# A linear-attention and gated-layer kernel: when the norms of four row tiles are asked for at the end of the second attention layer

## The chip, the cores and the metric

The kernel runs on one core of a Trainium2 chip. A core has five engines that run side by side and wait for each other through semaphores: TensorE (PE) multiplies matrices into the banks of PSUM, VectorE (DVE) and ScalarE (ACT) work on rows in SBUF and PSUM, GpSimd (POOL) works on SBUF, and SyncE (SP) issues most of the transfers (DMAs). The metric is the time of one execution on the device in microseconds (us); lower is better.

## The reference, cut to what matters

Four layers follow each other on x of 2048 rows by 1024 columns. Layers 0 and 2 are linear attention with 32 heads, layers 1 and 3 a gated feed-forward layer of width 3584. Each takes a layer norm of x and adds its result to x.

```
x = x + _A_ref(_layernorm(x), A_wqkv, A_wo)               # layer 0
x = x + _B_ref(_layernorm(x), B_W_gate, B_W_up, B_W_down) # layer 1
x = x + _A_ref(_layernorm(x), A_wqkv, A_wo)               # layer 2
x = x + _B_ref(_layernorm(x), B_W_gate, B_W_up, B_W_down) # layer 3

_layernorm(x) = (x - mean(x)) / sqrt(var(x) + 1e-5)       # per row
_A_ref: pq, pk = phi(q), phi(k);  kv = sum_s pk v;  z = sum_s pk
        o = (pq kv) / (pq z + 1e-6);  returns o @ wo
_B_ref: h = relu(x W_gate) * (x W_up);  returns h @ W_down
```

The place of the change is the end of layer 2 and the start of layer 3: the rows that layer 2 has just completed are normed for layer 3.

## The kernel before

**Tiles.** x lies in SBUF as 16 tiles of 128 rows (tile t), four of which are a quarter. Layer 2 ends with the product of the scaled queries `pqT` and the matrix `T` (the folded output weights). For quarters 0 and 1 `out_unit` (L792) makes one half of a tile at a time: eight matmuls into one PSUM bank, which DVE then adds onto x with `add_up` (L787; its instruction stands under L788), summing the row as it does so. Quarter 0 runs by columns, first the left halves of tiles 0 to 3 and then the right halves, quarter 1 by rows. Quarter 2 is made in pairs of tiles by `products` (L836), a scheme of seven products numbered m = 1, 5, 2, 6, 3, 7, 4, which saves matmuls by adding blocks before and after (`sums_T` and `sums_q` make the blocks, under L553). Quarter 3 waits for layer 3 to run.

**Banks.** The units of quarters 0 and 1 and four banks of `products` share a pool of four PSUM banks, so that a unit can start only when DVE has emptied the bank of the unit four before it. Two more banks, `oy`, take the products m = 6, 7 and 4 in turn.

**The norm of a tile** has four parts. `ln_norm_sums` (L217) lets DVE make the negative mean from the row sums of both halves (L224), and ACT the sum of squares (L227), then Ln and Exp (L228, L229) for `rstd`. Its inner `scale` makes the scaled rows `xnb`: for tiles 1 to 4 of layer 3 on DVE (L233), for the others on ACT (L236, L237). `ln_turn` (L411) has SP issue a DMA that transposes them into `xnT` (L416). With tile j of quarter 0 and tile 4 + j of quarter 1 both transposed, `sums_x` (L1150) adds and subtracts their blocks on DVE (L1160 to L1163). `glu` (L1172) reads `xnT` and these sums.

**What sets the order.** `_Later` (L71) holds tasks by tick; every output unit of L974 and of the loop at L975, and each of the seven products of quarter 2, is followed by one tick, and tasks due at one tick run in the order in which they were registered. `ln_at` (L418) asks for a tile's statistics after `delay` ticks, for its scaling one tick later and for its transpose `lag` ticks after that; `ln_later` (L434) does so for four tiles, `step` ticks apart. On DVE and POOL the order of these requests is the order of the instructions, since `manual_schedule` covers this stretch (L950). On PE, ACT and SP a planner orders the instructions by its own estimate of when each is ready; where two are ready the one asked for first goes first. Every engine runs its list in order.

Between the same ticks SP is given other transfers. `free_slowly` (L967) loads layer 3's first weights at ticks 1, 3 and 5 after L967 (gate weights under L1083, their block sums under L1086). `bring` (L959) fetches tiles of x that had been sent to DRAM, two each at what are ticks 5 and 7 after L973 (L279). The norms of quarter 1 are asked for at L978, at ticks 7, 9, 11 and 14 counted from L973, and `sums_x` at ticks 16, 18, 20 and 21 (L979). The first sums of the left-over blocks stand at ticks 1, 3 and 5 (L971).

Of the kernel before, what the change touches and what calls it, by code (L numbers as in the profile page):

```python
# [92 lines left out]
class _Net:  # L93
# [380 lines left out]
    def layer_A(self, l, last_ln):  # L474
# [253 lines left out]
        def z_mult(sc, j):  # L728
            prod = ksum
            nc.gpsimd.tensor_tensor(out=prod, in0=pq_of[sc, j], in1=zrow, op=ALU.mult)  # L730
            if l and sc == self.NQ - 1:
                later.at(6, lambda: self.behind(self.last_put, lambda _: z_sum(prod, sc, j), (0,)))
            else:
                later.at(2, lambda: z_sum(prod, sc, j))
# [26 lines left out]
        def q_turn(sc, j):  # L761
            if sc not in pqT:
                pqT[sc] = self.slot(f"pqT{l}_{sc}")
            self.last_turn = nc.sync.dma_start_transpose(out=pqT[sc][:, :, j * P:(j + 1) * P],
                                                         in_=pq_of[sc, j])

        def fold_wo(n):

            n2, a = divmod(n, H)
            if n2 == 0:  # L770
                T.append(self.slot(f"T{l}_{a}", [P, 4, D]))
            ps = [pool.tile([P, NW], F32, tag=tag, name=f"fold{l}_{n}_{i}") for i, (pool, tag) in
                  enumerate(((self.kvp, "kv0"), (self.kvp, "kv1"), (self.ps3, "b"), (self.ps3, "b")))]
            wo = ring.get((l, f"o{n2}"))
            for b in range(R):
                g = a * R + b
                for i in range(R):
                    e = slice(i * HD, (i + 1) * HD)
                    nc.tensor.matmul(ps[i][b * HD:(b + 1) * HD, :], lhsT=kvT[e, g, e],
                                     rhs=wo[e, g, :], start=True, stop=True,  # L780
                                     tile_position=(i * HD, b * HD))
            for i in range(R):
                g = a * R + i
                dst = T[g // 4][:, g % 4, n2 * NW:(n2 + 1) * NW]
                nc.scalar.activation(out=dst, in_=ps[i], func=ACT.Copy)
# [90 lines left out]
        def column_major(f, q):  # L876
            return [lambda j=j, c=c: f(q, j, c) for c in range(H) for j in range(QT)]

        def row_major(f, q):
            return [lambda j=j, c=c: f(q, j, c) for j in range(QT) for c in range(H)]  # L880

        def run(*lists):

            n = max(len(u) for u in lists)
            for i in range(n):
                for u in lists:
                    if i < len(u):
                        u[i]()
                        later.tick()
# [60 lines left out]
        with self.tc.manual_schedule(engines={mybir.EngineType.DVE, mybir.EngineType.Pool}):  # L950
            q3 = row_major(q_unit, self.NQ - 1)
            out0 = column_major(out_unit, 0)
            bring = self.bring_back if l else self.load_x
            ring.load_to(ring.index((l, "v1")) + 1)
            m_products(q3.pop(0))
            q3.insert(0, lambda: None)
            later.at(1, lambda: self.behind(ring.last, bring, range(self.NS)))
            for t in range(self.NS, self.ST - QT, 2):
                later.at((8 if l else 10) + t, lambda t=t: self.behind(self.last_turn, bring, (t, t + 1)))  # L959

            def with_fold(u, i):
                return lambda: (u(), fold_wo(i // 2) if i % 2 == 0 else None)

            run(q3[:2])
            run([with_fold(u, i) for i, u in enumerate(q3[2:] + out0[:1])])
            run(out0[1:3])
            ring.free_slowly((l, "o0"), later, 2)  # L967
            sums_T, sums_q, products = out_pairs()
            for i in range(11, 11 if l else self.ST):
                later.at(1 + 3 * (i - 11), lambda i=i: z_mult(*divmod(i, QT)))  # L970
            for n, at in enumerate((1, 3, 5) if l else ()):  # L971
                later.at(at, lambda n=n: self.behind(self.last_x, sums_T, (n,)))
            self.ln_later(last_ln, 0, 2, 2, 2)  # L973
            run(out0[3:])  # L974
            for sc in range(1, self.NQ - 1):  # L975
                if sc == 1:
                    for j in range(QT):
                        self.ln_at((2, 4, 6, 9 if l else 8)[j], last_ln, QT + j, 2, lambda j=j: self.last_seed if l and j == 3 else None)  # L978
                        later.at((11 if l else 12, 13, 15, 16)[j], lambda j=j: self.behind(  # L979
                            self.last_x, lambda j: self.sums_x(last_ln, 0, j), (j,)))  # L980
                if sc == 1 and l == 0:
                    for w, n in (("g", 3), ("u", 11)):
                        later.at(n, lambda w=w: self.behind(
                            self.last_x, lambda w: self.make_gu(ring.get((last_ln, 0, w, 0)), w, 0), (w,)))
                if sc == 1 or l == 0:
                    for n in range(4 if l else 0):
                        later.at(3 + n, lambda n=n: self.behind(self.last_x, lambda n: sums_q(2, (n,)), (n,)))
                    run(row_major(out_unit, sc))
                else:
                    self.behind(self.last_x, sums_T, (3,))  # L990
                    products(sc, 1)
            self.pairs = (lambda ns: [sums_T(n) for n in ns], lambda: sums_q(self.NQ - 1),
                          lambda: products(self.NQ - 1, 2))
            self.late_z = [lambda j=j: z_mult(self.NQ - 1, j) for j in range(QT)] if l else []
            self.turns = [lambda j=j: q_turn(self.NQ - 1, j) for j in range(QT)] + [
                lambda t=t: self.behind(self.last_turn, bring, (t,)) for t in range(self.ST - QT, self.ST)]
# [606 lines left out]
```

## Time and profile before

| What | us |
|---|---|
| median of 3 runs | 1450.57 (1449.26 to 1451.74) |
| the profiled execution | 1449.07 |
| its span, first to last instruction | 1447.3 |
| PE busy | 1437.4 |
| DVE busy | 964.6 |
| ACT busy | 606.7 |
| POOL busy | 312.1 |

The profile is one execution, taken by the hardware's profiler; its span is 1.8 us shorter than its time, because something lies before the first and after the last instruction. Times in the views are counted from the start of the span. A line of the order of time gives the start, the length, the engine, the line of the kernel, the operation and the tiles (out<-in); square brackets give how long the engine had stood idle and what ended it. "SPq" marks SP's queue: its length is the time that the issue held SP, not the transfer's.

### The profile page before, as it was taken

To read this page: it belongs to the slowest core of one execution; us is meant where nothing else is said; L and a number is where in the kernel's file an instruction comes from. 1 tells how busy PE (TensorE), PEld (TensorE's weight loads), DVE (VectorE), ACT (ScalarE), POOL (GpSimd) and SP (SyncE) were. 2 spreads that over 40 slices of the span, in tenths; PEclk is the share of its full clock that TensorE was granted. 3 is DMA by queue.
4 is the path that set the end of the run, shared out by engine and by line. 5 is a ranking of instruction groups with operands and counts; after the bars stand their busy time and mean duration, and the time that the engine had idled before them with its cause. 6 is when DMAs were issued, how large, how long until landed. Compare 5 with 4: busy or idle time off the path is not lost.

```text
span 1447.3 us, 20243 instructions
## 1 busy us (share of the span) xinstructions
PE 1437.4 (99%) x7422; PEld 708.0 (49%) x7422; DVE 964.6 (67%) x1795; ACT 606.7 (42%) x1101; POOL 312.1 (22%) x221
## 2 busy tenths in 40 slices
PE   9999999999999999999999999999999999999998
PEld 4444444444455444445654444444444574444457
DVE  7978698777594456549678876855545864444595
ACT  7872563333333334332068626532333433333300
POOL 1453861011100011110031587040111011111002
PEclk9999999999999999999999999999999999999999
DMA  9950787898469999636973119859843799444465
GB/s 285 238 161 8 175 210 209 278 338 262 157 219 307 352 290 306 201 128 222 295 238 95 59 30 254 241 168 327 254 146 129 218 296 323 146 145 146 153 234 181
DMA packets 328836, 304.90 MB, mean 211 GB/s; under 512 B 107456, under 2 KB 291776, under 8 KB 327712
## 3 DMA queue, kind: packets, MB, share of 16 engines
q1 hardware_dynamic: 320688, 282.30, 65.3%
q10 hardware_dynamic: 6560, 17.24, 3.1%
q0 software_dynamic: 1488, 4.07, 0.8%
q8 instruction: 58, 0.95, 0.3%
q14 instruction: 42, 0.34, 0.1%
HBM read 227.28 MB, written 51.64 MB: 193 GB/s over the span
## 4 chain that ended last, share of the span: by engine, by line
PE 92%; DVE 4%; ACT 2%; issue 1%; DMA 1%; POOL 0%; DVEq 0%; ACTq 0%
PE ps L500 11%; PE yu L1187 10%; PE yg L1187 10%; PE dy L1307 8%; PE xu L1187 7%; PE xg L1187 7%; PE dx L1307 6%; PE vg L1187 3%; PE zu L1187 3%; PE zg L1187 3%; PE vu L1187 3%; PE my L582 3%; PE dyT L1359 2%; PE mx L582 2%; PE mv L582 2%; PE dy L1359 2%
## 5 line engine op out<-in xcount | busy, mean ns | idle before, releaser
L1187 PEld LDWEIGHTS <-w 128*128 128x128 f16 (+1 forms) x3136 | 306.7, 98 | 372.5 <-issue 3.7
L1247 POOL TENSOR_TENSOR h<-m5u,m5g 128x512 f16<-128x512 f32 x56 | 73.0, 1303 | 717.3 <-DVE m5u L1243 615.2
L500 PE MATMUL ps<-w,xnT 128*128 128x512 bf16 x768 | 170.0, 379 | 0.5 <-ACT xnT L354 0.2
L1230 DVE TENSOR_TENSOR zg<-yg,m5g 128x512 f32<-128x512 f32 x56 | 39.1, 699 | 195.3 <-PE yg L1187 191.4
L500 PEld LDWEIGHTS <-xnT 128*128 128x128 bf16 x768 | 74.2, 98 | 90.4 <-issue 1.8
L1187 PE MATMUL xu<-xnT,w 128*128 128x512 f16 x448 | 115.1, 379 | 0.0
L1187 PE MATMUL yu<-s,w 128*128 128x512 f16 x448 | 114.9, 379 | 0.1
L1187 PE MATMUL xg<-xnT,w 128*128 128x512 f16 x448 | 115.0, 379 | 0.0
L1187 PE MATMUL yg<-s,w 128*128 128x512 f16 x448 | 114.9, 379 | 0.0
L1307 PEld LDWEIGHTS <-h 128*128 128x128 f16 x672 | 65.8, 98 | 78.2
L1359 PEld LDWEIGHTS <-h 128*128 128x128 f16 x966 | 94.5, 98 | 12.3
L443 ACT ACTIVATE e<-e,eps 128x512 f32<-128x512 f32 x128 | 91.0, 720 | 3.2
L730 POOL TENSOR_TENSOR kvc<-pq,kvc 128x1024 f32<-128x1024 bf16 x32 | 78.5, 2454 | 58.0 <-DVE den L744 35.1
L1195 ACT ACTIVATE m5g<-m5g 128x512 f32<-128x512 f32 x56 | 35.1, 627 | 124.2 <-DVE m5g L1243 124.2
L1307 PE MATMUL dx<-w,h 128*128 128x512 bf16 x392 | 85.3, 379 | 0.0
L1211 ACT ACTIVATE m5g<-vg 128x512 f32<-128x512 f32 x56 | 33.4, 597 | 100.9 <-PE vg L1187 100.9
L521 POOL TENSOR_TENSOR kvc<-kvc,slab 128x512 f32<-128x512 f32 x46 | 57.2, 1250 | 76.0 <-DVE slab L446 72.7
L1198 DVE TENSOR_TENSOR h<-yu,r 128x512 f16<-128x512 f32 x56 | 38.6, 690 | 50.3 <-PE yu L1187 50.3
L796 PE MATMUL ps<-T,pqT 128*128 128x512 bf16 x320 | 69.7, 379 | 0.0
L1195 ACT ACTIVATE r<-yg 128x512 f32<-128x512 f32 x56 | 33.4, 597 | 84.8 <-PE yg L1187 84.8
L1195 ACT ACTIVATE r<-zg 128x512 f32<-128x512 f32 x56 | 32.8, 586 | 80.9 <-PE zg L1187 73.3
L442 ACT ACTIVATE e<-ps 128x512 f32<-128x512 f32 x92 | 54.3, 590 | 29.2 <-PE ps L500 28.3
(238 smaller groups left out, 2405.6 us busy)
## 6 DMA issues: line engine op xcount, KB each, us to landing
w<-in_B_W_gate_dram SPq DMA_DIRECT2D x56, 512.0 KB, 6.6
w<-in_B_W_up_dram SPq DMA_DIRECT2D x56, 512.0 KB, 5.9
w<-tg SPq DMA_DIRECT2D x42, 512.0 KB, 7.5
w<-tu SPq DMA_DIRECT2D x42, 512.0 KB, 6.6
w<-ddT SPq DMA_DIRECT2D x21, 896.0 KB, 6.5
w<-td SPq DMA_DIRECT2D x18, 896.0 KB, 5.2
w<-dd SPq DMA_DIRECT2D x15, 896.0 KB, 5.4
w<-in_B_W_down_dram SPq DMA_DIRECT2D x14, 896.0 KB, 4.8
```

What stands on the lines that cost most here:

```text
L442: nc.scalar.activation(out=e, in_=ps, func=ACT.Relu, scale=-1.0)
L443: self.last_exp = nc.scalar.activation(out=e, in_=e, func=ACT.Exp, scale=-1.0, bias=self.eps6[:, 0:1])
L500: nc.tensor.matmul(by_row(ps), lhsT=self.xnT[l, l_q][:, kt, j * P:(j + 1) * P], rhs=w[:, kt, :].rearrange("p (b i d) -> p i b d", i=R, d=H ...
L521: nc.gpsimd.tensor_tensor(out=ksum[:, cols], in0=ksum[:, cols], in1=pk, op=ALU.add)
L582: nc.tensor.matmul(banks[j], lhsT=A(i)[:, j * P:(j + 1) * P], rhs=B(i), start=start and i == 0, stop=i == NS - 1, skip_group_check=True)
L730: nc.gpsimd.tensor_tensor(out=prod, in0=pq_of[sc, j], in1=zrow, op=ALU.mult)
L796: nc.tensor.matmul(ps, lhsT=pqT[sc][:, g, j * P:(j + 1) * P], rhs=T[g // 4][:, g % 4, n2 * NW:(n2 + 1) * NW], start=(g == 0), stop=(g == G ...
L1187: nc.tensor.matmul(ps, lhsT=W[w][m][:, k, :], rhs=A[m][:, k, :], start=start and k == 0, stop=k == 3, skip_group_check=True)
L1195: self.last_relu = nc.scalar.activation(out=out, in_=ps, func=ACT.Relu)
L1247: self.last_h = nc.gpsimd.tensor_tensor(out=h[:, 3, :], in0=V["u"], in1=V["g"], op=ALU.mult)
L1307: nc.tensor.matmul(banks[j], lhsT=A(k)[:, j * P:(j + 1) * P], rhs=w[:, i, :], start=start and k == 0, stop=k == self.U - 1, skip_group_che ...
L1359: nc.tensor.matmul(bank[:, j * H:(j + 1) * H], lhsT=A[i // 2][:, i % 2, j * P:(j + 1) * P], rhs=B[m][:, i, :], start=start and i == 0 and ...
```

## The change

One call is changed. In layer 2 alone (`l` is 2; in layer 0 the old values stay) the four tiles of quarter 0 are asked for one tick apart, at ticks 2, 3, 4 and 5 in place of 2, 4, 6 and 8, and each transpose one tick after the scaling in place of two. The scalings so move from ticks 3, 5, 7, 9 to 3, 4, 5, 6 and the transposes from 5, 7, 9, 11 to 4, 5, 6, 7.

```
-            self.ln_later(last_ln, 0, 2, 2, 2)
+            self.ln_later(last_ln, 0, 2, 1 if l else 2, 1 if l else 2)
             run(out0[3:])
```

`run(out0[3:])` holds the last five units of quarter 0, so that ticks 1 to 5 follow these and ticks 6 to 13 the units of quarter 1.

## The prediction

> **What bounds the kernel now.** I read four views in this order: the page's busy line, the waits of TensorE (PE) around the change, VectorE's (DVE's) instructions in order of time there, and SyncE's (SP's) queue. The busy line says how much can be gained at all:
>
> ```profile
> PE 1437.4 (99%) x7422; PEld 708.0 (49%) x7422; DVE 964.6 (67%) x1795; ACT 606.7 (42%) x1101; POOL 312.1 (22%) x221
> ```
>
> PE is busy for 1437.4 of 1447.3 us, so an edit counts only where PE stands still. PE's waits from 890 to 940 us (engine and line <- what it waited for: total, times, longest):
>
> ```profile
> PE oy L864 <- DVE x L852: 1.8, 1, 1.8
> PE oy L864 <- DVE x L788: 0.5, 1, 0.5
> PE ov L864 <- DVE x L788: 0.4, 1, 0.4
> PE ox L864 <- DVE x L788: 0.2, 1, 0.2
> ```
>
> All are waits for DVE to empty a PSUM bank. By the starts of the matmuls, 0.216 us apart when nothing holds them, PE loses 0.19, 0.35 and 0.59 us at 916.7, 917.9 and 919.4, then 1.95 at 928.2 and 0.66 at 932.1: 3.74 us, 0.26% of the span. That is the most a perfect edit of this place can give. DVE's order of time shows what makes it late (start, length, what; in brackets its idle time before):
>
> ```profile
> 906.53 0.81 DVE L233 TENSOR_SCALAR xnb<-x,mv,rstd 128x1024 f16<-128x1024 f32 x1 [0.33 <-ACT rstd L229]
> ...
> 910.98 0.81 DVE L233 TENSOR_SCALAR xnb<-x,mv,rstd 128x1024 f16<-128x1024 f32 x1 [2.05 <-ACT rstd L229]
> ...
> 923.01 0.69 DVE L788 SCALAR_TENSOR_TENSOR x<-ox,x 128x512 f32<-128x512 f32 x1
> ...
> 926.00 0.42 DVE L1160 TENSOR_TENSOR s<-xnT 128x512 f16<-128x512 f16 x1 [2.29 <-DMA xnT<-xnb]
> ```
>
> Twice DVE stands before a scaling (L233) for ScalarE's (ACT's) rstd, 2.38 us together; then, with its adds done at 923.70, 2.29 us for a transpose to land before the first sums of layer 3 (L1160). The adds behind that wait (L852) hold PE at 928.2. SP's queue:
>
> ```profile
> 907.72 0.90 SPq L279 DMA_DIRECT2D x<-away  x2
> 908.72 0.64 SPq L1083 DMA_DIRECT2D w<-in_B_W_gate_dram  x1
> 909.40 1.42 SPq L1086 DMA_DIRECT2D w<-tg  x1
> 910.93 3.85 SPq L416 DMA_TRANSPOSE xnT<-xnb  x1
> 914.82 1.05 SPq L279 DMA_DIRECT2D x<-away  x2
> 915.97 12.38 SPq L416 DMA_TRANSPOSE xnT<-xnb  x7
> ```
>
> The transpose of tile 0, whose scaled rows ACT had finished at 904.79, goes out only at 910.93, behind the loads asked for before it. The eight go in the order of their ticks, 0, 1, 2, 4, 3, 5, 6, 7; the first sums need tiles 0 and 4. By the trace's semaphore updates the fourth, tile 4, was issued at 921.17 and landed at 925.91.
>
> [...] all loads and transposes from 906 to 930 us landed in the order of issue, so a transpose moved ahead pushes what it overtakes back. [...] the squares (L227) took 1148. [...] The trace has such a packet at 923.56 (934 ns), and the transposes' packets nearly stop from 924.1 to 925.3. [...] here it fell on tile 4's transpose.
>
> **The change part by part.** It adds and removes no instruction. Ticks are output units from L973 on. Statistics of tiles 0 to 3 go from ticks 2, 4, 6, 8 to 2, 3, 4, 5, scalings from 3, 5, 7, 9 to 3 to 6, transposes from 5, 7, 9, 11 to 4, 5, 6, 7.
>
> *DVE, whose order is written out.* Before, an add and a 1.59 us sum (L553) stood between mean 1 (L224, 903.88) and scaling 1 (906.53). Now scaling 1 follows an add and mean 2, ready at about 904.3. It needs rstd 1. ACT must still do tile 0's shift and scaling (0.29 + 1.24) and square 1 (1.15 + 0.19), Ln (0.29) and Exp (0.20): from 903.2 that is 906.5, as now. But mean 2 is there by then, and the planner does not put Ln straight behind its square when another square is ready: squares of tiles 2 and 4 at 908.11 and 909.26 both ran before their Ln at 910.39. I take the same here: square 1 at 904.70 plus the 2.87 us from 908.11 to scaling 2 at 910.98 gives scaling 1 at 907.6, idle 3.3 us; bounds 905.3 (square 1 before tile 0's scaling) and 907.8. Then the add and sum run, mean 3 ends at 910.6, and scaling 2 has its rstd: idle 0. Scaling 3 has only scaling 2 (0.73) and an add (0.65) behind mean 3; its chain needs 1.9: idle 0.55. Scaling 4 has an add and a sum (1.3) behind its mean: idle 0.65, where it had none. Sum of DVE idle: 4.5 against 2.38, so DVE is 2.1 us later at the last out_unit add (919.22 becomes 921.3).
>
> *Who waits for that.* Behind each scaling on DVE stand the adds that free PE's four banks. Unit (4,0) is drained at 911.9 instead of 907.95 and unit (6,0) on its bank wanted to start at 909.59: PE loses about 2.2 us there that it does not lose now, and the products (L864) start 2.1 to 2.2 later.
>
> *What it hides behind.* Before, DVE reached the first sums at 923.70 and stood until 926.00. Now it arrives at 923.70 + 2.2 = 925.9. The stall is paid at the scalings instead of at the transpose. If this cover were gone (tile 4 already landed before), the 2.2 us would be a plain loss.
>
> *SP and the DMAs.* All eight transposes still go out; tile 0's passes four transfers (two bring-backs, gate weights and their sums), tiles 1 and 2 pass the second pair of bring-backs, tile 3 passes tile 4. Service times from the packets: transposes 0.92 us, bring-backs 1.3, gate weights 1.75, sums 1.3. From 911.25, when the up weights are through: tile 0 912.2, two bring-backs 914.8, gate and sums 917.9, tiles 1 and 2 919.8, two bring-backs 922.4 (landed 923.2; 921.24 before), tile 3 923.3, tile 4 924.3, landed about 925; with the pause up to 926.3. So tile 4, now fifth in line, is hardly earlier than 925.91. The delayed bring-backs feed L852, which DVE now reaches at about 923.3: hidden, by 0.1 us; without DVE's lag they would hold it. The weights passed are for later units: hidden. POOL's queue is not touched.
>
> *Sum.* First sums at 926.0 (before 926.00); sums 1.47, first L852 0.68: the bank is free at 928.2 (before 928.15), but PE ends the products before it at 919.36 + 2.2 + 4 x 1.73 = 928.5, so m = 7 starts at 928.5 (928.21). The last product waits for the DVE chain from the first sums, 932.1 as before. PE's losses up to m = 7: 0.19 + 0.35 + 0.59 + 1.95 = 3.08 before, 1.13 + 2.2 = 3.3 after, of which the shorter wait of the last product gives most back. Between 0 and +0.3 I take +0.1: span 1447.4, execution 1449.2 against 1449.07; the median shown, 1450.57, is 1.5 above the profiled execution, so 1450.7. Bounds: first sums at 925.0 (rstd 1 early, tile 4 landing without the pause) give -1.0; at 927.0 (DVE's wait longer, or the pause on tile 4) +1.0.
>
> **Rivals.** (a) Faster: the transposes do come early and DVE no longer waits. For: SP sat on tile 0 for 6 us, and the pause may move off tile 4. Against: tile 4 stays behind the same bytes, and the second bring-backs land later. It saves the 1.95 us at 928.2: 1448.6; with the smaller stalls up to all 3.74: 1446.8. (b) Slower, small: ACT puts another square ahead of rstd 3 and rstd 4 too, 3.1 us from mean to scaling as for tile 2, +1.0 each: 1452.6. (c) Slower: SP holds tile 4. A transpose issued behind a full queue took 1.88 to 3.85 us on SP instead of 1.25. With tiles 2 and 3 just ahead, tile 3 may take 3.85 from 919.6 and tile 4 3.12, then 3.5 to land as before: 930.1 instead of 926.0, all paid by PE behind L852: +4.1, 1454.7. It decides from a landing at 928.9 on. Against: the bytes ahead are through by 923. (d) The planner keeps the old order of SP and ACT: 1450.6.
>
> **How the numbers follow.** A measurement of this kernel can tell about 0.2%, 2.9 us, from no change. Likeliest case 0.58, own range 1449.6 to 1451.7; (a) 0.18, of which 0.08 beyond 2.9 us; (b) 0.10; (c) 0.11; (d) 0.03. So faster 0.08, slower 0.11, same 0.81. Cutting off most of (c) and the far part of (a) leaves 1448.0 to 1453.6.
>
> **What would show it.** Right: idle of about 3 us before the first L233 and little before L1160, out units of PE waiting for L788 from about 909.6, no wait for L852 at m = 7. Tile 0's transpose at about 907.7, the second bring-backs after tiles 1 and 2. Wrong: L233 waits under 1 us, or tile 4 landing before 924 or after 928, or another order of PE between products and layer 3's first matmuls, which could fill PE's stall.

## The result and the profile after

The changed kernel takes 1452.51 us (median of 22 runs, 1451.20 to 1453.82) against 1450.38 us before (22 runs, 1448.94 to 1451.74). The ratio is 1.0015 with a 95% interval of 1.0009 to 1.0022: 2.1 us slower. That is clear of the noise, but below the 0.2% that the prediction set as its bound for "no change". The profiled execution took 1452.42 us, with a span of 1450.6 us, against 1449.07 and 1447.3 before. The predicted time was 1450.7 us. One execution of the last kernel below, which took 2166.26 us at a mean clock of 0.654, is left out of all comparisons.

The busy line of the page, after:

```profile
PE 1439.2 (99%) x7422; PEld 708.7 (49%) x7422; DVE 964.5 (66%) x1795; ACT 606.3 (42%) x1101; POOL 312.0 (22%) x221
```

The instruction counts are those of before. TensorE (PE) is 1.8 us busier with the same 7422 matmuls, so some of them took longer. PE's waits from 890 to 940 us, the same stretch as before (engine and line <- what it waited for: total, times, longest):

```profile
PE oy L864 <- DVE x L852: 2.2, 1, 2.2
PE ps L796 <- DVE x L788: 1.7, 2, 1.0
PE ov L864 <- DVE x L788: 0.4, 1, 0.4
```

The second line is new: two output units now wait for VectorE (DVE), as forecast. The first line should have gone, and grew from 1.8 to 2.2 us. DVE in order of time (start, length, what; in brackets the idle time before):

```profile
907.59 0.81 DVE L233 TENSOR_SCALAR xnb<-x,mv,rstd 128x1024 f16<-128x1024 f32 x1 [3.22 <-ACT rstd L229]
...
912.14 0.81 DVE L233 TENSOR_SCALAR xnb<-x,mv,rstd 128x1024 f16<-128x1024 f32 x1 [0.54 <-ACT rstd L229]
...
915.68 0.81 DVE L233 TENSOR_SCALAR xnb<-x,mv,rstd 128x1024 f16<-128x1024 f32 x1 [0.66 <-ACT rstd L229]
...
924.91 0.69 DVE L852 TENSOR_TENSOR x<-x,ov 128x512 f32<-128x512 f32 x1 [1.04 <-PE ox L864]
...
928.30 0.43 DVE L1160 TENSOR_TENSOR s<-xnT 128x512 f16<-128x512 f16 x1 [1.48 <-DMA xnT<-xnb]
...
929.78 1.28 DVE L852 TENSOR_TENSOR x<-x,oy 128x512 f32<-128x512 f32 x2
```

The three idle times before the scalings (L233) are the forecast ones. Not forecast is that DVE still stands, 1.48 us, before the first sums of layer 3 (L1160), and that these start at 928.30 instead of 926.00. The add at 924.91 also stood 1.04 us; the view puts that down to PE, but by the semaphores its last release was the brought-back tile, which landed at 924.82. SyncE's (SP's) queue:

```profile
907.76 0.42 SPq L279 DMA_DIRECT2D x<-away  x1
908.30 1.61 SPq L416 DMA_TRANSPOSE xnT<-xnb  x1
909.96 0.58 SPq L279 DMA_DIRECT2D x<-away  x1
910.63 0.44 SPq L1083 DMA_DIRECT2D w<-in_B_W_gate_dram  x1
911.12 2.62 SPq L1086 DMA_DIRECT2D w<-tg  x1
913.84 5.18 SPq L416 DMA_TRANSPOSE xnT<-xnb  x2
919.07 1.05 SPq L279 DMA_DIRECT2D x<-away  x2
920.22 8.08 SPq L416 DMA_TRANSPOSE xnT<-xnb  x4
```

Tile 0's transpose goes out 2.6 us earlier than before, though behind the first bring-back, the second pair of bring-backs 4.25 us later (919.07 against 914.82). By the semaphore updates the last group is tile 3, tile 4, tile 5, tile 6; tile 4 was issued at 921.56 (921.17 before) and landed at 928.28 (925.91 before). So four transposes did go out sooner, and the one that DVE waits for landed 2.37 us later.

PE in order of time at that place, first before, then after:

```profile
928.21 1.89 PE L864 MATMUL oy<-T,pqT 128*128 128x512 f16 x8 [1.78 <-DVE x L852]
...
932.10 1.89 PE L864 MATMUL oy<-sR,pqT 128*128 128x512 f16 x8 [0.49 <-DVE x L788]
```

```profile
930.51 3.45 PE L864 MATMUL oy<-T,pqT 128*128 128x512 f16 x8 [2.17 <-DVE x L852]
933.75 1.19 PE L1187 MATMUL xg<-xnT,w 128*128 128x512 f16 x4
934.78 0.81 PE L1187 MATMUL xu<-xnT,w 128*128 128x512 f16 x3
935.43 0.81 PE L864 MATMUL oy<-sR,pqT 128*128 128x512 f16 x3
```

The eight matmuls of product m = 7 (oy<-T,pqT) take 3.45 us; before, the same group took 1.89. The last product is oy<-sR,pqT. The table by stretches says why (the stretch and its length; busy us and instructions of PE, PEld, DVE, ACT, POOL; then PEclk, the clock granted to TensorE; the share of the DMA engines; GB/s):

```profile
927.26:930.67 3.41, 1.24 (x7) 0.49 (x5) 2.33 (x6) 0.57 (x1) 0.00 (x0) 1.00 0.80 170
930.68:934.08 3.40, 3.40 (x9) 1.22 (x8) 3.37 (x10) 0.00 (x0) 0.00 (x0) 0.50 1.14 331
```

From 930.67 us PE ran at half its clock for 3.41 us, just after a stretch of the same length in which it had been busy for 1.24 us only. The profile before has no such stretch in the whole kernel except at its very end (from 1445.85 us on).

So the profiled pair splits as follows. Product m = 7 starts 2.30 us later (930.51 against 928.21). From there to the last product it was 3.89 us and is 4.92 us: +1.03, namely the slow matmuls less the wait before the last product, which is gone. From the last product to the last matmul both have 511.4 us. Together +3.33 us, and the spans differ by 3.3. This pair overstates the change, since the medians differ by 2.1 us only: the profiled execution of the kernel before has no half clock inside, while the mean clock of about half of its executions is below 1.000 (see the table below).

### The profile page after: what moved, and what is told of

It is laid out like the page before. It is cut to its first block, busy times and chain, and to the rows that moved or that the text cites. A ratio compares the mean times of both kernels' runs of the same rounds, so it can differ in the third digit from the quotient of the medians.

```text
span 1450.6 us, 20242 instructions
## 1 busy us (share of the span) xinstructions
PE 1439.2 (99%) x7422; PEld 708.7 (49%) x7422; DVE 964.5 (66%) x1795; ACT 606.3 (42%) x1101; POOL 312.0 (22%) x221
## 4 chain that ended last, share of the span: by engine, by line
PE 90%; DVE 4%; ACT 3%; issue 1%; DMA 1%; POOL 0%; SPq 0%; DVEq 0%; ACTq 0%
PE yu L1187 10%; PE yg L1187 10%; PE ps L500 10%; PE dy L1307 7%; PE xg L1187 7%; PE xu L1187 7%; PE dx L1307 6%; PE vg L1187 3%; PE zu L1187 3%; PE vu L1187 3%; PE zg L1187 3%; PE my L582 3%; PE dyT L1359 2%; PE mv L582 2%; PE mx L582 2%; PE dy L1359 2%
```

## The experiments

Theory A: what the change costs comes from tile 4's transpose, which SP's queue now lands later; DVE's own lag is covered. Theory B: the loss is DVE's waits for rstd, or the waits of the output units that they cause. Later runs add theory C, that the half clock follows from PE's wait, and D, that it comes by itself. Every ratio is to the kernel before on the same chip and in the same job. This table is read through the paragraphs below it. "Below 1.000" counts the executions whose mean granted clock was under 1.000. The column before the last is the median of the others: an execution at 1.000 cannot have had a stretch like the one above, since 3.41 us at half clock alone take the mean over 1450 us to 0.9988. That column compares kernels without the half clock, but coarsely, since the two sets of the kernel before already lie 0.6 us apart in it. For the kernel before both columns are taken over three later jobs, the median over the first.

| kernel | tile 4 landed | m = 7 starts | PE's wait there | last product | below 1.000 | median at 1.000 | median us |
|---|---|---|---|---|---|---|---|
| before | 925.91 | 928.21 | 1.78 | 932.10 | 56 of 110 | 1449.56 | 1450.38 |
| before again | 926.92 | 929.22 | 2.08 | 933.11 | 5 of 13 | 1450.14 | 1450.22 |
| the change | 928.28 | 930.51 | 2.17 | 935.43 | 15 of 22 | 1451.79 | 1452.51 |
| scalings alone | 927.84 | 930.14 | 1.47 | 934.03 | 1 of 13 | 1450.98 | 1451.03 |
| bring-backs together | 927.77 | 930.06 | 1.79 | 933.95 | 4 of 13 | 1450.73 | 1450.74 |
| scalings a tick later | 929.09 | 931.32 | 3.90 | 936.24 | 12 of 12 | none | 1453.04 |
| lag alone | 926.94 | 929.18 | 1.92 | 933.07 | 4 of 12 | 1449.35 | 1449.63 |
| tile 4 ahead | 926.19 | 929.12 | 0.91 | 933.02 | 1 of 12 | 1450.48 | 1450.42 |
| change, sums behind adds | 928.92 | 928.03 | 0 | 933.85 | 0 of 12 | 1450.24 | 1450.24 |
| before, sums behind adds | 926.70 | 926.66 | 0 | 931.69 | 2 of 20 | 1448.31 | 1448.24 |
| before, both sums behind | 927.24 | 926.85 | 0 | 930.77 | 2 of 19 | 1448.63 | 1448.63 |

Two things follow. The change costs 2.2 us among the executions at 1.000 (1451.79 against 1449.56) and 2.0 among those below (1452.86 against 1450.82), so the lower clock, which both kernels show, is only a small part of the difference of the medians. And a kernel that seldom shows it looks cheaper in its median than its delay would make it.

**The kernel before, once more.** Nothing is edited; it shows how far two profiles of one kernel differ.

> The kernel before, unchanged, for its clock records. If the slow stretch of PE's clock that the changed kernel's profile shows (3.4 us at half speed from 930.7 us on, 1.5 us lost) belongs to the change, all executions of this one have a mean granted clock of 1.000 and lie within about 0.7 us. If it belongs to this place whatever the change (an idle PE of about 2 us), some of these executions also show 0.998 to 0.999 and are some 1.5 us longer, and the two kernels differ by the 2.2 us that separate their faster halves. Median ratio 1.000 either way.

Measured: 1450.22 us, ratio 1.0000 (0.9992 to 1.0009). Of the two outcomes the second came: 5 of 13 executions were below 1.000, so such a clock is not the change's own. These 5 were only 0.4 us longer than the others; in the kernel before of the three jobs it is 1.3 us. In the profile tile 4 lands 1.0 us later than in the first one, 0.25 of which is a later start of this whole part. A single landing is therefore known to some 0.8 us only, and the differences below rest on the medians and on the order of events as well.

**The scalings alone.** The first number of the change, with the transposes left at their old ticks.

```
-            self.ln_later(last_ln, 0, 2, 1 if l else 2, 1 if l else 2)
+            for j in range(QT): self.ln_at((2, 3, 4, 5)[j] if l else 2 + 2 * j, last_ln, j, (2, 3, 4, 5)[j] if l else 2)
```

> Statistics and scalings at the new ticks 2 to 5 and 3 to 6, transposes at the old ticks 5, 7, 9, 11, so that SP issues all bring-backs in their old places (tile 3's transpose still goes out ahead of tile 4's). Theory A (the loss is the later landing of tile 4's transpose, through the order of SP's queue): DVE still idles 3.2 us at the first L233, yet tile 4 lands at about 925 to 926, the first sums start at 926.0 to 926.8, and the time is 0 to 0.8 us over before. Theory B (the loss is DVE's wait for rstd, passed on to PE): 2.2 us over before, as with the whole change.

Measured: 1451.03 us, ratio 1.0005 (0.9997 to 1.0013). DVE's waits for rstd are those of the change in full (3.23, 0.54 and 0.66 us), and so are the waits of the output units (1.7 us), and yet the median is only 0.6 us over before, though the interval reaches from -0.4 to 1.9. Among executions at 1.000 it is 1.4 us; the medians are closer because 1 of 13 had the lower clock, against 23 of 40 of the kernel before in this job. In SP's queue, up to tile 4, only tiles 3 and 4 have changed places. Tile 4 landed at 927.84, not at 925 to 926 as expected. DVE and PE at the place, DVE first:

```profile
927.93 0.42 DVE L1160 TENSOR_TENSOR s<-xnT 128x512 f16<-128x512 f16 x1 [1.98 <-DMA xnT<-xnb]
```

```profile
930.14 1.89 PE L864 MATMUL oy<-T,pqT 128*128 128x512 f16 x8 [1.47 <-DVE x L852]
934.03 1.89 PE L864 MATMUL oy<-sR,pqT 128*128 128x512 f16 x8 [0.50 <-DVE x L788]
```

DVE, though 2.2 us late from the scalings, still stood 1.98 us for tile 4. Its lag is covered, and m = 7 starts 1.93 us later than in the first profile because of the landing. The eight matmuls take 1.89 us: no half clock.

**The second bring-backs beside the first.** The change, with the second pair of bring-backs asked for at the tick of the first, so that tiles 1 and 2 no longer pass it.

```
-                later.at((8 if l else 10) + t, lambda t=t: self.behind(self.last_turn, bring, (t, t + 1)))
+                later.at(16 if l else 10 + t, lambda t=t: self.behind(self.last_turn, bring, (t, t + 1)))
```

> The change, but the second pair of bring-backs is asked for with the first, ahead of the transposes of tiles 1 and 2. Theory A, with the gap of 0.9 us in the second pair's packets as a part (issued only when the queue before them has run dry): the second L852 no longer waits, tile 4 lands 0.9 us or more earlier than 928.28, at 927.3, or at 925.8 if its packets then come through before PE's instruction fetch at 926.2; time 1.0 to 2.2 us under the change. Theory B: DVE idles 3.2 us as before at L233 and the time stays that of the change, 2.2 us over before.

Measured: 1450.74 us, ratio 1.0004 (0.9996 to 1.0012), which cannot be told from the kernel before. The second bring-backs land at 917.72 and 919.01 us, the add that stood 1.04 us no longer stands, and tile 4 lands at 927.77, 0.5 us earlier than in the change where 0.9 was expected. That takes back 1.8 of the 2.1 us in the median, 1.1 of 2.2 among executions at 1.000. The rest goes with the lower clock, which fewer executions had (4 of 13 against 15 of 22). How much of the 1.1 is the landing, one profile of each kernel does not tell.

**The scalings a tick later.** The change with each scaling two ticks after its statistics, and so each transpose a tick later too; the tick of the bring-backs and of the third weight load are moved as well, which was meant to keep SP's order. The main lines of the edit, against the kernel before:

```
-            self.later.at(1, lambda: norm(scale))
+            self.later.at(mid, lambda: norm(scale))
...
+            for j in range(QT): self.ln_at(2 + j if l else 2 + 2 * j, last_ln, j, 1 if l else 2, None, 2 if l else 1)
```

> Statistics at the new ticks 2 to 5, scalings two ticks after them (4 to 7) and transposes at 5 to 8, with the bring-backs and the third weight load a tick later too, so that SP's queue keeps the order of the change up to the swap of the gate weights and tile 0. DVE does an add, a sum and a mean more before each scaling: its idle at the first L233 falls from 3.2 to under 1 us. Theory A: tile 4's transpose has the same transfers ahead of it and lands at 927 to 928.3 all the same; DVE waits for it 3 to 4 us instead of 1.5; time 1.5 to 2.2 us over before. Theory B: the loss goes with the wait, 0 to 0.3 us over before.

Measured: 1453.04 us, ratio 1.0020 (1.0012 to 1.0029). DVE's wait before the first scaling fell from 3.22 to 1.23 us (under 1 was expected) and the two waits of output units at 909 to 912 us are gone, but the kernel is no faster than the change. SP's order is not quite that of the change: here the second of the first two bring-backs goes ahead of tile 0. Tile 4 lands at 929.09, and PE pays for all of it:

```profile
931.32 2.72 PE L864 MATMUL oy<-T,pqT 128*128 128x512 f16 x8 [3.90 <-DVE x L852]
```

This speaks plainly against B: more than half of DVE's waits at the scalings was mended (4.4 us fell to 1.9) and the loss stayed, because it only moved to the wait for tile 4. PE is at half clock for 3.41 us here too.

**The lag alone.** The second number of the change, on the kernel before.

```
-            self.ln_later(last_ln, 0, 2, 2, 2)
+            self.ln_later(last_ln, 0, 2, 2, 1 if l else 2)
```

> Edit: the first layer is as before, and in the second the four norms stay two output units apart as before, but each transpose is asked for one step behind its scaling, as in the change. This is the change's second number alone. Compiled, VectorE's order is that of before, and SyncE's is tile 0, tile 1, second bring-backs, tile 2, tile 4, tile 3, so tile 4's transpose stays ahead of tile 3's. Theory A (what the change costs is tile 4's transpose landing late, because SyncE reaches it late): tile 4 lands within 0.8 us of before (925.1 to 926.7 us), TensorE waits for line 852 by no more than 2.0 us and no stretch at half speed follows, so 1450.0 to 1450.9 us. Rival B (any step of a transpose ahead of the bring-backs and weight loads costs, whatever tile 4 does): 1451.5 us or more.

Measured: 1449.63 us against 1450.01 in this job, ratio 0.9997 (0.9988 to 1.0005). Tile 0's transpose passes three transfers, tile 1's the second bring-backs, and tile 4 stays ahead of tile 3. This part began 0.84 us later than in the first profile of before (first bring-back 908.56 against 907.72); with that taken off, tile 4 lands at 926.1 against 925.91. Here transposes asked for earlier cost nothing as long as tile 4 kept its place.

**Tile 4 ahead of tile 3.** The change, with tile 3's transpose asked for later and made to follow tile 4's in SP's order. The lines added, against the kernel before, the transpose's arguments left out:

```
+        with self.tc.issue_after(self.t4.ins) if (layer, t) == (3, 3) else nullcontext(): it = nc.sync.dma_start_transpose(...); self.t4 = it
...
+            for j in range(QT): self.ln_at((2, 3, 4, 5)[j] if l else 2 + 2 * j, last_ln, j, (1, 1, 1, 5)[j] if l else 2)
```

> Edit: the changed kernel with tile 3's transpose asked for after tile 4's and made to wait in SyncE's order for it, so SyncE issues tile 4's ahead of tile 3's; all else as in the change. Theory A: tile 4 lands one transpose (0.92 us) earlier, near 927.3 us instead of 928.28; VectorE stands about 0.5 us before its first sums instead of 1.48; TensorE waits for line 852 about 1.3 us instead of 2.17. Theory C beside it [...]: no half-speed stretch, so the time falls by 0.9 us and by the stretch's 1.5 us, to 1450.3 us (1449.8 to 1451.2). Rival D (the half-speed stretch comes by itself, not from the wait): 1451.6 us, half of the runs still with a clock of 0.998. Rival B (the loss is TensorE's waits at the output units 909 to 914 us): 1452.5 us, unchanged.

Measured: 1450.42 us, ratio 1.0002 (0.9994 to 1.0011). With two transposes exchanged, the median cannot be told from the kernel before (0.4 us over it), while the waits of the output units (1.7 us) are still there. Tile 4 landed at 926.19, more than one transpose earlier and 1.1 us earlier than expected; that part is luck, because PE's packet of instructions, behind which the transposes nearly stopped in the profiles before and after (13 and 19 GB/s), came at 926.30 here, just after tile 4's landing. DVE then no longer stands before the sums:

```profile
926.31 0.69 DVE L788 SCALAR_TENSOR_TENSOR x<-ox,x 128x512 f32<-128x512 f32 x1
...
926.92 0.42 DVE L1160 TENSOR_TENSOR s<-xnT 128x512 f16<-128x512 f16 x1
```

Only in this kernel, among those with the old order on DVE, is DVE itself what sets the sums. That leaves a remainder: m = 7 starts 0.91 us later than in the first profile of before, and the executions at 1.000 are 0.9 us over. DVE comes late to the sums by its lag and by 1.16 us that it stood for the second bring-backs (landed at 925.00). With tile 4 out of the way, DVE's lateness is no longer covered. In the other seven profiles, whatever DVE and PE had done before, product m = 7 starts 2.23 to 2.30 us after tile 4's landing (from the table: 928.21 - 925.91 = 2.30, and so on to 931.32 - 929.09 = 2.23). That constancy, and the loss that went with the exchange, are the evidence for theory A.

**The sums behind the adds, on the change.** The first sums are asked for one product later (tick 12 for 11 in the code, which counts from five ticks later than the text above), so that the two adds of product m = 6 (L852) go ahead of them on DVE and free PE's banks.

```
-                        later.at((11 if l else 12, 13, 15, 16)[j], lambda j=j: self.behind(
+                        later.at((12 if l else 12, 13, 15, 16)[j], lambda j=j: self.behind(
```

> Edit: the changed kernel with the sums over the first pair of transposed tiles asked for one product later (tick 12 instead of 11), so that on VectorE the two adds of the sixth product stand ahead of them. VectorE then no longer stands for tile 4's transpose with those adds queued behind it. Theory A: TensorE's wait for line 852 of 2.17 us is gone (0 to 0.3 us), with no half-speed stretch; part comes back ahead of the last product, whose banks the sums now hold up by about 1.2 to 1.5 us. The last product then starts near 933.1 us instead of 935.43, and the time is 1450.3 us (1449.6 to 1451.0). Rival B (the loss is TensorE's waits at the output units 909 to 914 us): 1452.5 us, unchanged. If the sums themselves are what is late for the feed-forward layer, the waits come back after 933 us and the time is 1452 to 1453 us.

Measured: 1450.24 us, ratio 1.0004 (0.9995 to 1.0012). PE:

```profile
928.03 1.89 PE L864 MATMUL oy<-T,pqT 128*128 128x512 f16 x8
...
933.85 1.89 PE L864 MATMUL oy<-sR,pqT 128*128 128x512 f16 x8 [1.77 <-DVE x L788]
```

Product m = 7 starts without a wait although tile 4 landed at 928.92, later than in the change. Of the wait taken away, 1.77 us come back before the last product, a little more than the 1.2 to 1.5 expected. No execution had a clock below 1.000.

**The sums behind the adds, on the kernel before.** The same line changed in the kernel before.

> Edit: the kernel before, with the same move of the first sums behind the sixth product's two adds (tick 12 instead of 11) and nothing else. Theory A: in the kernel before, too, the 1.95 us that TensorE stands ahead of the seventh product are paid for tile 4's transpose (VectorE stood 2.29 us for it). They go, about 0.8 us come back ahead of the last product, and the time is 1449.2 us (1448.6 to 1450.0), faster than both kernels. Rival: what the adds gain, the sums and the last product's banks lose: 1450.4 us.

Measured: 1448.24 us (20 runs) against 1450.01 in the same job, ratio 0.9988 (0.9982 to 0.9995): faster than both kernels, and more so than the 1449.2 us expected. Among executions at 1.000 the gain is 1.25 of the 1.8 us; the rest goes with the lower clock, which only 2 of 20 had, against 20 of 47 of the kernel before in this job. PE's waits from 903 to 945 us, and DVE at the place:

```profile
PE oy L864 <- DVE x L788: 1.0, 1, 1.0
PE ov L864 <- DVE x L788: 0.6, 1, 0.6
PE ox L864 <- ACT oy L868: 0.3, 1, 0.3
PE ox L864 <- DVE x L788: 0.2, 1, 0.2
PE vg L1187 <- DVE s L1160: 0.2, 1, 0.2
```

```profile
924.27 0.69 DVE L852 TENSOR_TENSOR x<-x,oy 128x512 f32<-128x512 f32 x1 [0.16 <-PE oy L864]
925.13 0.69 DVE L852 TENSOR_TENSOR x<-x,oy 128x512 f32<-128x512 f32 x1 [0.18 <-PE oy L864]
926.79 0.42 DVE L1160 TENSOR_TENSOR s<-xnT 128x512 f16<-128x512 f16 x1 [0.97 <-DMA xnT<-xnb]
```

DVE stands for the same transpose, for 0.97 us, but nothing that PE wants is queued behind it any more. The wait for L852 has left the list.

**The second sums behind the adds as well.** Ticks 12, 14, 15, 16 in place of 11, 13, 15, 16 on the kernel before, so that the adds of m = 7 go ahead of the second sums.

> Edit: the kernel before with the first sums asked for one product later (as in the run before this one) and the second sums one product later as well (ticks 12, 14, 15, 16), so that the two adds of the seventh product stand ahead of the second sums on VectorE. What is asked: whether the 1.15 us that TensorE still stood ahead of the last product are worth anything. Theory A1 (the next bound is that wait): the last product starts near 930.5 us instead of 931.69 and the time falls by about 1 us more, to 1447.2 us. Rival A2 (VectorE itself is now the bound: from 926.79 to 936.9 us it stood only about 0.6 us, so the sums that the feed-forward products need come out when they did): the wait moves to the first feed-forward product that reads sums, and the time is 1447.7 to 1448.4 us, the same as with the first sums alone.

Measured: 1448.63 us (19 runs) against 1450.45 in its job, ratio 0.9984 (0.9977 to 0.9991). The interval overlaps that of the run before it for the most part, so the second move adds nothing that shows. The last product did start earlier, as A1 said (930.77 instead of 931.69), but gained nothing by it: in PE's order it now stands behind three matmuls of the feed-forward layer instead of ten, the other seven come after it, and the first product that reads the sums starts at 935.30 against 935.04. The outcome is A2's; of its reason the profile shows the one half, that the sums' readers start when they did, but not a wait in front of them.

## Why the prediction was right or wrong

*Class and range.* "Same" by the bound of 0.2% was right (+0.15%), and 1452.51 lies in the range. The central value was 1.8 us short, and the likeliest case's own range (1449.6 to 1451.7) missed it. That the class held is in part luck: the bound of 2.9 us is wider than the 2.1 us that the prediction did not see. Of its own signs, "no wait for L852 at m = 7" did not come, and "tile 4 landing after 928", a sign of being wrong, did.

*The DVE step: right.* Scaling 1 at 907.6 with 3.3 us idle was forecast; 907.59 and 3.22 came. For scalings 2, 3 and 4, 0, 0.55 and 0.65 us against 0, 0.54 and 0.66. The reason given, that ScalarE puts square 2 ahead of Ln 1, is what the trace shows: squares at 904.73 and 905.86, both Ln from 906.99. *Who waits for that: nearly right.* PE loses 1.17 and 0.86 us at 909.06 and 911.65, 2.03 us where 2.2 was forecast in one place.

*What it hides behind: right in kind, short by 0.9 us.* DVE's adds were done at 926.82, not 925.9. The second pair of bring-backs, called hidden "by 0.1 us", was not: it landed at 924.82 instead of 923.2, and L852 stood 1.04 us.

*SP and the DMAs: the step that failed.* The order was right but for one item without effect on tile 4 (tile 0's transpose passed three transfers, not four: the first bring-back stayed ahead of it). The landing was mis-sized: "about 925; with the pause up to 926.3" measured 928.28. The step laid service times end to end from 911.25 and took the queue for never empty. Of tile 4's 2.37 us over before, 1.77 were there when the nine transfers that both kernels have ahead of it had landed (924.82 against 923.05); the other 0.60 came with tile 3's transpose, now ahead of it too. The 1.77 are mostly two places where the queue ran dry, by the packets' rates about 0.5 us near 911.5 and 0.95 us at the second bring-backs (estimates). The latter in the table by stretches (last column GB/s):

```profile
918.40:920.40 2.00, 2.00 (x10) 0.88 (x9) 1.96 (x7) 1.87 (x6) 0.00 (x0) 1.00 1.21 287
920.40:921.40 1.00, 0.57 (x4) 0.19 (x2) 1.00 (x4) 1.00 (x2) 0.00 (x0) 1.00 1.13 135
921.40:923.40 2.00, 2.00 (x10) 0.88 (x9) 1.91 (x5) 1.97 (x7) 0.00 (x0) 1.00 0.89 324
```

SP, held 2.86 us at tile 2's transpose, issued these loads at 919.07, when the packets before them ended at about 920.4. Their first packets took some 0.9 us each instead of about 0.16, so the rate fell to 135 GB/s. Before, the same loads were issued at 914.82 with the work of 4 us still queued, and nothing showed. That the late issue is the cause is read from the trace; no run moved it alone. The pause behind PE's instruction packet was foreseen and taken only as a bound; with PE's lag of 2.2 us the packet moved from 923.56 to 926.18, and behind it tile 4's packets nearly stopped again:

```profile
926.60:927.90 1.30, 1.30 (x8) 0.59 (x6) 0.22 (x2) 1.23 (x1) 0.00 (x0) 1.00 1.24 19
```

*Sum: right once the landing is put in.* With tile 4 at 928.28, the sum's own way of counting (first sums at 928.30, sums 1.47, first add 0.68) gives m = 7 at 930.45, and 930.51 came. So the landing carries the miss: m = 7 was forecast at 928.5. One more term had no price in the sum, what PE does after such a wait. In the profiled pair the half clock adds 1.03 us at the last product, as in the run with scalings a tick later (4.92 us from m = 7 to the last product; 3.89 or 3.90 in the five other kernels that keep the old order on DVE). In the medians it is a small part, as said under the table.

*Rivals.* (c), SP holding tile 4, was nearest in its outcome: tile 4 took 3.12 us on SP, as it had guessed, and tile 3 only 1.23 instead of 3.85. But tile 4 was issued only 0.39 us later than before, so the hold is not what made it late. (a) did not come, since tile 4 never gained. (b) did not come: rstd 3 and 4 were as forecast. (d) did not come.

## What to carry to other kernels

Ask for the one transfer that a consumer waits for before moving its neighbours: here four transposes went out sooner and the fifth, the only one on the path, paid for them, while exchanging two of them gave most of it back. When an engine stands for a transfer, look at what stands behind it in its list; moving two ready adds ahead of the waiting sums was worth more (1.8 us below the kernel before) than any change to the transfer, none of which came clearly below it. And price a wait of TensorE of about 2 us with a possible stretch at half clock behind it: here 3.41 us of it followed the waits of 2.17 and 3.90 us, and with 1.78 to 2.08 us 69 of 148 executions had a mean clock below 1.000. Where executions come in two groups of clock, compare the groups as well as the medians.

## What the runs showed of the hardware

**Half clock after a short wait.** In the two profiles that have it inside the kernel, PE ran at half its clock for 3.41 us (in the change its matmuls are 0.43 us apart there instead of 0.216) after waits of 2.17 and 3.90 us. The nine other profiles, with waits of 0 to 2.08 us at m = 7, all have a mean clock of 1.000. The table's column shows that it goes with the wait: with waits of 0 to 1.47 us ahead of m = 7, 6 of 76 executions had a clock below 1.000; with 1.78 to 2.08 us, 69 of 148; with 2.17 us, 15 of 22; with 3.90 us, all 12. (A mean clock below 1.000 can also come from the end of the kernel, where the profiles before and after are at half clock from 1445.85 and 1449.50 us on.) In the kernel before, executions at 1.000 had a median of 1449.56 us and those below it 1450.82 (110 runs), so about half of its executions may well pay some 1.3 us for the same wait (an estimate from these two medians); which stretch of theirs was slow is not recorded.

In the clock records of the profiles before and after, every stretch that ends inside the kernel is a whole number of 3.4133 us long: in the change 925.01 us at full clock, 3.41 at half and 515.41 at full (271, 1 and 151 times), before 1440.42 us at full clock (422 times). Divided into pieces of this length from the start of the record, the change has PE busy for 22% of the piece from 1446.09 us and for 36% of the one from 927.26 us, ahead of the slow matmuls (1.24 of 3.41 us), and before for 31% of the one from 1442.44 us. Half clock follows each of these three. The next lowest, 70% in the change and 65% before, are followed by full clock. The 65% are the piece from 927.03 us, in which PE stood 1.18 us; the rest of its 1.78 us of waiting lies in the piece ahead of it (82% busy). Whether it is this share that decides, no run tested.

**Transposes nearly stop behind an instruction packet.** Behind a single packet of 16,384 bytes in the page's q8 instruction queue, which took 998 ns from 926.18 us on, the transposes' rate fell from 278 to 19 GB/s for 1.3 us (926.60 to 927.90), and rose to 271 GB/s after it. Before the change the same happened behind the packet at 923.56 us (934 ns): 13 GB/s for 1.2 us (924.10 to 925.30), between 254 and 248. The packet came when PE had started 9385 of its matmuls and weight loads before the change and 9391 after it, so here it goes with PE's progress, though it is 2.63 us later. It need not hit the transfer that matters: in the run with tile 4 ahead the packet came 0.11 us after the landing.
